# Attention and mixture kernel on one core: adding DMAs in the first quads, sums placed later, new drain counts, 33 plain steps

## Chip, core and metric

One core of a Trainium2 chip runs the whole program. The time is device microseconds of one execution, the median of several; a profiled execution of the same program gives the trace. The engines are TensorE (PE, with its weight loads PEld), VectorE (DVE), ScalarE (ACT), GpSimd (POOL) and SyncE (SP, which here only issues DMAs).

## What is computed

```python
B, N, C = 4, 6080, 256                    # q, k, v: [B, N, C], f32
qn = q / (norm(q, axis=1) + 1e-6); kn = k / (norm(k, axis=1) + 1e-6)
s = kn.transpose(0, 2, 1) @ qn / tau      # [B, C, C], a sum over all N tokens
a = softmax(s)                            # over the last axis
x = (v @ a).reshape(B * N, C)
h = x @ w_in                              # 256 -> 2048
out = (h - tanh(h)) @ w_out               # 2048 -> 256, f32
```

## The kernel before

The softmax matrix of a batch is folded into `w_in`, so the work on the tokens is (v times the folded weights), then h - tanh(h), then `w_out`. Each f32 operand is split into a high and a low part, and a product is three matmuls (high x low, high x high, low x high).

The tokens of a batch are taken in 6 pairs of column blocks (512 + 512, one pair 512 + 448), and the 2048 hidden channels in 8 slices of 256. One pair and one slice is a **quad**: a 2 x 2 product done by a seven-product scheme (`p1` to `p7`, banks X, Y, Z, tiles `x`, `y`, `z` in the trace). There are 4 x 6 x 8 = 192 quads, numbered `gs` from 0. A quad of the name `b_p_s` is batch, pair, slice. From a product TensorE hands a PSUM bank to ScalarE (`keep`, tiles `p1`, `u2`, `u3`), VectorE adds (`add`, tiles `c11`, `c22`, `c12`), ScalarE takes tanh, the tanh is subtracted (`sub`, or `join`), ScalarE casts the high part (`gh`), VectorE subtracts for the low part (`gl`), and TensorE multiplies with `w_out` (`second`, tiles `ps_o`).

How far these second products trail is `lag`: `ORDER`, `UNEVEN` and `HALVES` give the order of the seven products in a quad, and after each the number of second matmuls that are drained there. The quads of the last batch except its first pair (`halved`, `gs` 152 to 191) do also the first output column by a seven-product scheme on half blocks of 256 columns (tiles `ps_h`, sums `ts`, parts `b1`, `b2`, `t1`, `t2`); their banks Y and Z are the same one, so that `p5` (into Y) has to wait until VectorE has added `c11` out of Z. The sums of `w_out` for it (`Sums`, `plan_sums`) are made beforehand, eight of them, at quads `SUMS_AT` to `SUMS_AT + 7`.

Where `joined` says so, the subtraction is no VectorE instruction: ScalarE takes tanh(-h), and GpSimd issues a DMA that adds h onto it in SBUF (`join`). In the kernel before these are hidden blocks 11 and 12 of the 40 halved quads, 80 DMAs.

The inputs `w_in` and `w_out` are 64-bit floats; `Convert` turns a slice into a high and a low f32 part, with an addition `add` on the way (GpSimd's at first, VectorE's where `alone`: slices 1 to 7 of `w_out` and slice 7 of `w_in`).

The scores of batch 0 are done at the start by plain f32 matmuls (`score`), of the later batches by split matmuls, in units of one token tile and one half of the channels (`score_unit`). Of batch 1 the first `FILLS` of 48 token tiles are done by plain matmuls too (tiles `ps_s<-qh` and `ps_s<-ql`), put by the planner where TensorE would wait; the rest are units, six per quad at most (`PER`), in quads 17 to 22.

All instructions are recorded in a `Plan`; a list scheduler with costs written in the kernel (`order`) decides the order on each engine, and the program then runs in that order, in order on each engine. The planner takes a join to cost 1.0 on GpSimd and to be seen 4.5 plus 0.19 later (`JOIN_LAG`).

Of the kernel before, what the change touches and what calls it, by code (L numbers as in the profile page):

```python
# [15 lines left out]
ALU = mybir.AluOpType  # L16
AX = mybir.AxisListType

P = 128
# [22 lines left out]
UNEVEN = [  # L42
    ("p6", [2]), ("p2", ["c"]), ("p5", []), ("p7", [12]), ("p3", ["a"]), ("p4", ["d", 3]), ("p1", ["b", 7]),
]
HALVES = [
    ("p6", []), ("p2", [5, "c"]), ("p5", []), ("p7", [5]), ("p4", ["d", 3]), ("p3", ["a", 4]), ("p1", ["b", 5.5]),
]
HALF = NMAX // 2
LAST = 1
SHARE = 1  # L50
JOINED = [(),(11,12)]
SUMS_AT = 3 * 8
ENTER = 10
EARLY = 6
FILLS = 35
FILL_EVERY = 0.6
LEAD = 10
KEPT = 50.0
# [189 lines left out]
def act_cost(n):  # L248
    return 0.09 + n * 0.00084


def dve_cost(n):
    return 0.068 + n * 0.001042


def pool_cost(n):
    return 0.27 + n * 0.0022


def pe_cost(n):  # L260
    return 0.0134 + n * 0.000417
# [3 lines left out]
def attn_moe(ctx: ExitStack, tc: tile.TileContext, qk, v4, qkT, tau, w_in, w_out, outT):  # L265
# [6 lines left out]
    nc = tc.nc  # L272
    B, N, _, C = qk.shape
# [8 lines left out]
    while s0 < N:  # L282
        n = min(NMAX, N - s0)
# [24 lines left out]
    def sb(pool, tag, shape, dtype, name):  # L308
        return pool.tile(list(shape), dtype, tag=tag, name=name, bufs=ring[tag].bufs)

    def bank(i, name, shape=(P, 512)):

        return ps_p.tile(list(shape), F32, tag=f"bank{i}", name=name)
# [38 lines left out]
    class Convert:  # L352
# [29 lines left out]
            nc.vector.scalar_tensor_tensor(self.mf, self.low.bitcast(U32), 2.0 ** -52, self.mf, op0=ALU.mult, op1=ALU.mult)  # L382

        def add(self, eng):
            eng.tensor_add(self.af, self.af, self.mf)

        def hi(self):
            nc.scalar.copy(self.h, self.af)
# [116 lines left out]
    while j < NJ:  # L505
        n = min(GJ, NJ - j) if j else NJ % GJ or GJ
# [13 lines left out]
    def units_of(left):  # L520
        return [(m, g, jj) for m in range(KC) for g in [*left[:1], *left[-1:], *left[1:-1]] for jj in range(groups[g][1])]
# [4 lines left out]
    class Attn:  # L526
        def __init__(self, b):
# [9 lines left out]
            self.half, self.unit = {}, {}  # L537
            self.units = units_of(range(steps[FILLS][0] if b == SWEEP else 0, len(groups)))

# [59 lines left out]
        def score(self, g, jj):  # L599
# [4 lines left out]
            for m in range(KC):  # L604
                products(
                    self.ps[:, m, :], [((x[:, K_COLS[m]], None), (x[:, Q_ALL], None))],
                    first=i == 0 and m == 0, last=i == (FILLS if self.b else len(steps)) - 1 and m == KC - 1,
                )
# [349 lines left out]
    plan = Plan()  # L958
# [101 lines left out]
    def plan_convert(conv, dst, after=(), due=None, alone=False):  # L1060

        adds = ("DVE", dve_cost(WN), nc.vector) if alone else ("POOL", pool_cost(WN), nc.gpsimd)
        raw, c, t = Buf(ring["raw"]), Buf(ring["nt"]), Buf(ring["ob"])
        plan.add("SP", 0.35, conv.load, writes=[raw, dst], after=after, size=0.52, due=due)
        plan.add("ACT", act_cost(WN), conv.magnitude, reads=[raw], writes=[c])
        plan.add("DVE", 1.07, conv.upper, reads=[raw], writes=[c])
        plan.add("DVE", 1.06, conv.lower, reads=[raw, c], writes=[t])
        plan.add(*adds[:2], lambda: conv.add(adds[2]), reads=[t], writes=[c])
        plan.add("ACT", act_cost(WN), conv.hi, reads=[c], writes=[dst])
        plan.add(*adds[:2], lambda: conv.lo(adds[2]), reads=[c], writes=[dst])  # L1070

# [2 lines left out]
    def plan_w_in(s, due=None, after=(), alone=False):  # L1074
        w = wbuf[0, s] = Buf(ring["wi"])
        plan_convert(convert_w_in(s), w, after, due, alone)
        w.writers[-1].due = plan.pe_time - 0.5
        if s > EARLY:
            plan_keep(s, w)
        return w  # L1080
# [25 lines left out]
    def halved(b, p):  # L1106

        return b == B - 1 and p > 0
# [7 lines left out]
    class Quad:  # L1116
# [185 lines left out]
            stream.append((self, i))  # L1302

        def joined(self, i):
            return self.b == B - 1 and i in JOINED[halved(self.b, self.p)]

        def product(self, name):
            if name == "p1":
# [113 lines left out]
    def second(quad, i):  # L1422

        if isinstance(i, str):
            yield from second_halves(quad, i)
            return
        b, p, s = quad.b, quad.p, quad.s
        row, c = i // 10 - 1, i % 10 - 1
        n = quad.ns[c]
        f = 2 * s + row  # L1430
        gh, gl = quad.bufs["g", i]
        key = b, p, c
        first = key not in obufs
        if first:
            obufs[key] = [0] + [Buf(3 + 2 * c + m) for m in range(KC)]
        done = obufs[key]
        done[0] += 1
        last = done[0] == 2 * NS2

        parts = (0, 1, 0, 0), (0, 0, 0, 1), (1, 1, 0, 0), (1, 0, 0, 1), (1, 0, 1, 2), (0, 0, 1, 2)  # L1440
        end = last and b == B - 1 and p == NP - 1
        if end:
            parts = parts[0:2] + parts[5:6] + parts[2:5]
        for m, part, x, j in parts:
            def run(m=m, part=part, x=x, j=j):
                if first and j == 0:
                    outs[key + (m,)] = bank(3 + 2 * c + m, f"ps_o_{b}_{p}_{c}_{m}")
                nc.tensor.matmul(  # L1448
                    outs[key + (m,)][:, 0:n], (wo_l if part else wo_h)[:, f, m * P:(m + 1) * P], quad.g[i][x],
                    start=first and j == 0, stop=last and j == 2, skip_group_check=True,  # L1450
                )

            plan.add("PE", pe_cost(n), run, reads=[gl if x else gh, wobuf[s]], writes=[done[1 + m]])
            yield 1
        if last:
            at_ = b * N + pairs_of[b][p][0] + c * quad.ns[0]
            for m in range(KC):
                halves = b == B - 1
                ob = Buf(ring[("t" if halves else "raw") if c else "ob"])
                tiles = {}  # L1460

                def copy(m=m, tiles=tiles):
                    if halves:
                        tag = "t" if c else "ob"
                        tiles[0] = sb(g_p, tag, [P, NMAX], F32, f"ob_{b}_{p}_{c}_{m}")[:, 0:n]
                    elif c:
                        raw = sb(qk_p, "raw", [P, GJ, 2, C], F32, f"ob_{b}_{p}_{c}_{m}")
                        tiles[0] = raw[:, 0].rearrange("p x c -> p (x c)")[:, 0:n]
                    else:
                        tiles[0] = sb(g_p, "ob", [P, NMAX], F32, f"ob_{b}_{p}_{c}_{m}")[:, 0:n]  # L1470
                    (nc.scalar.copy if m else nc.vector.tensor_copy)(tiles[0], outs[key + (m,)][:, 0:n])  # L1471

                def store(m=m, tiles=tiles):
                    nc.sync.dma_start(outT[m * P:(m + 1) * P, at_:at_ + n], tiles[0])

                plan.add("ACT" if m else "DVE", act_cost(n) if m else dve_cost(n), copy, reads=[done[1 + m]], writes=[ob])
                plan.add("SP", 0.35, store, reads=[ob], size=0.26, due=plan.pe_time + 8.0)


    ats = {}  # L1480
# [2 lines left out]
    def task(gs, place, what):  # L1483
        beside.setdefault((gs, place), []).append(what)
# [162 lines left out]
    adds = 0  # L1647
# [12 lines left out]
    def plain_step(b, i, due=None):  # L1660
        g, jj = steps[i]
        if jj == 0:
            plain_load(b, g)

        return plan.add("PE", 2 * KC * 0.215, lambda: ats[b].score(g, jj), reads=held[b, g], writes=[scores[b]], due=due, fill=b == 1)
# [36 lines left out]

    fills = [plain_step(1, i, after_scores + FILL_EVERY * i) for i in range(FILLS)]

# [40 lines left out]
    for s in range(NS2):  # L1745
        task(SUMS_AT + s, "start", lambda s=s: plan_sums(s))
    for gs in range(halves_from, TOTAL):
# [17 lines left out]
    lag = LAG  # L1765
# [19 lines left out]
    for gs in range(TOTAL):  # L1785
        quad = quads.pop(gs)
        for what in beside.get((gs, "start"), ()):
            what()
        before, uneven = uneven, quad.ns[0] != quad.ns[1]
        if halves_from - 4 <= gs < halves_from:  # L1790
            lag += 3
        if gs == halves_from:
            lag += 2
        if before and not uneven:
            lag += ENTER if gs < halves_from else 0
            stream[-2:] = reversed(stream[-2:])
        for name, then in UNEVEN if uneven else HALVES if halved(quad.b, quad.p) else ORDER:
            if uneven and not before and name in ("p2", "p5"):
                drain(ENTER // 2)
            if name == "p1":  # L1800
                if gs + 1 < TOTAL:
                    quads[gs + 1] = Quad(gs + 1)
                    quads[gs + 1].product("p1")
            else:
                quad.product(name)
            for x in then:
                if not isinstance(x, str):
                    held = min(lag, x * SHARE if gs >= halves_from else x)
                    lag, x = lag - held, x - held
                    drain(x)  # L1810
                else:
                    for what in beside.get((gs, x), ()):
                        what()
# [66 lines left out]
```

## Time and profile before

| | us |
|---|---|
| time, median of 3 (lowest to highest) | 2145.12 (2145.1 to 2145.46) |
| time of the profiled execution | 2144.87 |
| its span, first to last instruction | 2143.1 |
| TensorE busy in it | 2135.9 |
| mean granted TensorE clock | 1.000 of 2.4 GHz |

The time holds 1.8 us that the span does not, and the profiled execution is 0.25 us under the median. Rows of the chain of work give a start, a length and what ran; rows of the timeline give start, length, engine, line, operation and, in brackets, the idle time of the engine before it with what ended it. Matmuls overlap, so the length of one matmul row says less than the distance between two starts.

### The profile page before, as it was taken

The numbers are of one execution on the slowest core, as the hardware profiler recorded it, in microseconds if no ns is written. First come the engines' busy times: TensorE is split into PE (matmuls) and PEld (weight loads), VectorE is DVE, ScalarE is ACT, GpSimd is POOL, SyncE is SP. The second block draws the span as 40 slices with busy tenths as digits, with TensorE's granted clock in tenths as the row PEclk, the third lists the DMA queues.
The fourth block names the chain that finished last, engine by engine and source line by source line (L and its number), as shares of the span: only waits on it lengthen the run. The fifth ranks groups of instructions, "written<-read, shape, count | busy, mean of one in ns | idle before, by whom it ended". The sixth has DMA issues, their size and how long they took to land.

```text
span 2143.1 us, 29494 instructions
## 1 busy us (share of the span) xinstructions
PE 2135.9 (100%) x10026; PEld 1802.5 (84%) x10026; DVE 1879.0 (88%) x3332; ACT 1616.3 (75%) x3015; POOL 106.2 (5%) x117
## 2 busy tenths in 40 slices
PE   9999999999999999999999999999999999999999
PEld 8888888888888888888888888888888888888887
DVE  8998988998898888888899888888888998988987
ACT  6677878767777787886777788887676777777776
POOL 5100000000000000000000000000000011111111
PEclk9999999999999999999999999999999999999999
DMA  9845676555335575643533567564353467877874
GB/s 384 303 165 194 214 253 222 189 181 184 127 135 187 212 245 212 219 162 108 199 138 126 180 231 246 196 227 158 110 197 125 156 207 204 230 230 205 231 209 136
DMA packets 143897, 419.73 MB, mean 196 GB/s; under 512 B 20674, under 2 KB 62914, under 8 KB 140674
## 3 DMA queue, kind: packets, MB, share of 16 engines
q1 hardware_dynamic: 132226, 396.87, 52.5%
q0 software_dynamic: 11520, 20.98, 5.4%
q8 instruction: 79, 1.29, 0.2%
q14 instruction: 72, 0.59, 0.1%
HBM read 329.19 MB, written 66.85 MB: 185 GB/s over the span
## 4 chain that ended last, share of the span: by engine, by line
PE 99%; DMA 1%; DVE 0%; SPq 0%; ACT 0%; issue 0%; ACTq 0%
PE ps_o L1448 43%; PE x L326 25%; PE y L326 12%; PE z L326 7%; PE ps_h L1371 5%; PE ps_s L326 3%; PE ps_s L653 2%; PE ps_s L651 1%; PE ps_w L326 1%; DMA n<-c 0%; DMA vhl<-qk_dram 0%; DVE c L1161 0%; DVE t L1285 0%; DVE v L955 0%; DVE gl L1293 0%
## 5 line engine op out<-in xcount | busy, mean ns | idle before, releaser
L326 PE MATMUL x<-v,f 128*128 128x512 f32 (+1 forms) x2304 | 628.2, 389 | 0.0
L1448 PE MATMUL ps_o<-gh,wo_h 128*128 128x512 f32 (+1 forms) x1376 | 533.6, 388 | 0.0
L1448 PE MATMUL ps_o<-gh,wo_l 128*128 128x512 f32 (+1 forms) x1376 | 533.5, 388 | 0.0
L326 PEld LDWEIGHTS x<-v,f 128*128 128x128 f32 x2304 | 430.1, 188 | 84.5
L1293 DVE TENSOR_TENSOR gl<-t,gh 128x512 fp32r<-128x512 f32 (+1 forms) x688 | 456.1, 679 | 20.9 <-ACT gh L1289 19.9
L1289 ACT CAST gh<-t 128x512 fp32r<-128x512 f32 (+1 forms) x688 | 412.2, 617 | 34.4 <-DVE t L1285 20.9
L1448 PE MATMUL ps_o<-gl,wo_h 128*128 128x512 f32 (+1 forms) x1376 | 428.0, 388 | 0.0
L1278 ACT ACTIVATE t<-c 128x512 f32<-128x512 f32 x536 | 333.8, 625 | 94.2 <-DVE c L1161 85.1
L1285 DVE TENSOR_TENSOR t<-c,t 128x512 f32<-128x512 f32 (+1 forms) x496 | 333.9, 677 | 24.7 <-ACT t L1278 19.5
L1151 ACT COPY u<-x 128x512 f32<-128x512 f32 (+1 forms) x384 | 221.9, 578 | 163.0 <-PE x L326 159.4
L1161 DVE TENSOR_TENSOR c<-u,y 128x512 f32<-128x512 f32 (+1 forms) x384 | 258.9, 674 | 76.3 <-ACT u L1151 47.9
L326 PE MATMUL y<-v,f 128*128 128x512 f32 (+1 forms) x1152 | 320.6, 387 | 1.1 <-DVE c L1161 1.0
L1448 PEld LDWEIGHTS ps_o<-gh,wo_l 128*128 128x128 f32 x1376 | 258.5, 188 | 51.4 <-DVE ob L1471 0.9
L1448 PEld LDWEIGHTS ps_o<-gl,wo_h 128*128 128x128 f32 x1376 | 258.2, 188 | 51.7 <-DVE gl L1293 0.6
L1448 PEld LDWEIGHTS ps_o<-gh,wo_h 128*128 128x128 f32 x1376 | 258.4, 188 | 49.1
L326 PEld LDWEIGHTS y<-v,f 128*128 128x128 f32 x1152 | 210.2, 188 | 36.2 <-DVE c L1161 1.8
L1161 DVE TENSOR_TENSOR c<-p,z 128x512 f32<-128x512 f32 x192 | 131.7, 686 | 36.3 <-PE z L326 33.5
L326 PE MATMUL z<-v,f 128*128 128x512 f32 x576 | 162.2, 390 | 0.0
L1278 ACT ACTIVATE t<-x 128x512 f32<-128x512 f32 x152 | 90.9, 598 | 92.7 <-PE x L326 91.1
L1285 DVE TENSOR_TENSOR t<-x,t 128x512 f32<-128x512 f32 x152 | 104.9, 690 | 45.4 <-ACT t L1278 44.9
L326 PEld LDWEIGHTS z<-v,f 128*128 128x128 f32 x576 | 108.1, 188 | 23.3 <-DVE t L1285 0.2
L1151 ACT COPY p<-x 128x512 f32<-128x512 f32 x192 | 112.7, 587 | 15.3 <-PE x L326 12.5
(215 smaller groups left out, 2191.4 us busy)
## 6 DMA issues: line engine op xcount, KB each, us to landing
f<-f_d SPq DMA_DIRECT2D x160, 896.0 KB, 4.6
raw<-qk_dram SPq DMA_DIRECT2D x104, 384.0 KB, 5.0
nt<-qkT_dram SPq DMA_DIRECT2D x96, 380.0 KB, 5.1
f_d<-f SPq DMA_DIRECT2D x32, 896.0 KB, 3.9
vraw<-v_dram SPq DMA_DIRECT2D x24, 1024.0 KB, 7.9
outT_dram<-ob SPq DMA_DIRECT2D x88, 256.0 KB, 3.2
sl<-so_d SPq DMA_DIRECT2D x40, 512.0 KB, 3.3
wt<-wt_d SPq DMA_DIRECT2D x24, 512.0 KB, 6.8
```

The source lines that it names most:

```text
L326: ins = nc.tensor.matmul(out, w, x, start=first and i == 0, stop=last and i == len(seq) - 1, skip_group_check=True,)
L651: nc.tensor.matmul(self.ps[:, 0:C], x[:, 1, k], x[:, 0, q], start=False, stop=last, skip_group_check=True)
L653: nc.tensor.matmul(self.ps.rearrange("p (a c) -> p a c", a=2), x[:, 0, k], x[:, :, q], start=first, stop=False, skip_group_check=True,)
L1151: nc.scalar.copy(self.tiles[to], self.tiles["X"][:, 0:n])
L1161: nc.vector.tensor_add(self.tiles[i], self.tiles[u], self.tiles[ps][:, 0:n])
L1278: nc.scalar.activation(self.tiles["t", i], self.tiles[c][:, 0:n], AF.Tanh, scale=-1.0 if apart else 1.0)
L1285: nc.vector.tensor_sub(x, self.tiles[c][:, 0:n], x)
L1289: nc.scalar.copy(self.g[i][0], self.tiles["t", i])
L1293: nc.vector.tensor_sub(self.g[i][1], self.tiles["t", i], self.g[i][0].bitcast(F32))
L1371: nc.tensor.matmul(outs[b, p, place][:, at_ * HALF:(at_ + 1) * HALF], weights(a, part), quad.g[name][x][:, half * HALF:(half + 1) * HALF], ...
L1448: nc.tensor.matmul(outs[key + (m,)][:, 0:n], (wo_l if part else wo_h)[:, f, m * P:(m + 1) * P], quad.g[i][x], start=first and j == 0, stop ...
```

## The change

It sets three tables anew (`HALVES`, `SUMS_AT` from quad 24 to quad 80, `FILLS` from 35 to 33), withholds one second matmul more at the first halved quad (`lag += 3` for `+= 2`), makes blocks 11 and 12 of quads 0 to 7 joined (16 DMAs more), makes the addition of the eight `alone` conversions an adding DMA (8 more), and lets ScalarE issue the store of the output block that it copied last.

```diff
-HALVES = [
-    ("p6", []), ("p2", [5, "c"]), ("p5", []), ("p7", [5]), ("p4", ["d", 3]), ("p3", ["a", 4]), ("p1", ["b", 5.5]),
-]
+HALVES = [("p6",[]),("p2",[5.5,"c"]),("p5",[]),("p7",[5.0]),("p4",["d",2.5]),("p3",["a",4]),("p1",["b",5.5])]
-SUMS_AT = 3 * 8
+SUMS_AT = 80
-FILLS = 35
+FILLS = 33
...
         def add(self, eng):
-            eng.tensor_add(self.af, self.af, self.mf)
+            if eng is None:
+                nc.gpsimd.dma_start(self.af, self.mf, accum_op=ALU.add)
+            else:
+                eng.tensor_add(self.af, self.af, self.mf)
...
+        far = alone and True
...
-        plan.add(*adds[:2], lambda: conv.add(adds[2]), reads=[t], writes=[c])
+        if far:
+            plan.add("POOL", 1.0, lambda: conv.add(None), reads=[t], writes=[c], port=False, lag=plan.JOIN_LAG)
+        else:
+            plan.add(*adds[:2], lambda: conv.add(adds[2]), reads=[t], writes=[c])
...
-            return self.b == B - 1 and i in JOINED[halved(self.b, self.p)]
+            return i in (JOINED[halved(self.b, self.p)] if self.b == B - 1 else (11,12,) if self.gs < 8 else ())
...
-                plan.add("SP", 0.35, store, reads=[ob], size=0.26, due=plan.pe_time + 8.0)
+                if end and m:
+                    plan.add("ACT", 0.1, lambda store=store: store(nc.scalar), reads=[ob])
+                else:
+                    plan.add("SP", 0.35, store, reads=[ob], size=0.26, due=plan.pe_time + 8.0)
...
         if gs == halves_from:
-            lag += 2
+            lag += 3
```

The tables go through the scheduler, so that what moves is seen only in the order of the instructions. ScalarE's rows in the first quad, before, from the tanh of block 11 (`t11_0_0_0`) to the cast of its high part (`gh11_0_0_0`):

```order
L1278 ACTIVATE t11_0_0_0_782<-c11_0_0_0_769 128x512
L1151 COPY u3_0_0_0_786<-x_0_0_0_728 128x512
L388 CAST wo_h_95<-a_wo3_714 128x512
L1278 ACTIVATE t22_0_0_0_797<-c22_0_0_0_791 128x512
L1278 ACTIVATE t21_0_0_0_810<-x_0_0_0_728 128x512
L1289 CAST gh11_0_0_0_815<-t11_0_0_0_782 128x512
```

The same stretch of ScalarE now (lines from 1156 on are five higher, and `u3_0_0_0` stands one row ahead of these):

```order
L1283 ACTIVATE t11_0_0_0_776<-c11_0_0_0_763 128x512
L891 CAST f_2_782<-fx_0_2_758 128x896
L1283 ACTIVATE t22_0_0_0_789<-c22_0_0_0_780 128x512
L1283 ACTIVATE t21_0_0_0_798<-x_0_0_0_718 128x512
L367 ACTIVATE a_wo4_803<-raw_wo4_676 128x512
L1156 COPY p1_0_0_1_809<-x_0_0_1_791 128x512
L1294 CAST gh22_0_0_0_812<-t22_0_0_0_789 128x512
L1294 CAST gh21_0_0_0_819<-t21_0_0_0_798 128x512
L1283 ACTIVATE t12_0_0_0_829<-c12_0_0_0_817 128x512
L1156 COPY u2_0_0_1_835<-x_0_0_1_791 128x512
L1294 CAST gh11_0_0_0_844<-t11_0_0_0_776 128x512
```

The cast of block 11 stands nine instructions behind its tanh where it stood four behind, and the second matmuls of block 11 are still the first on TensorE. VectorE's rows at the second halved quad (`3_1_1`) before, from the first that reads its joined block (`n11_3_1_1`) to the addition `c11` of the quad after:

```order
L1234 TENSOR_TENSOR ts_3_1_1_18131<-n11_3_1_1_18056 128x256
L1234 TENSOR_TENSOR ts_3_1_1_18131<-n21_3_1_1_18105,n11_3_1_1_18056 128x256
L1285 TENSOR_TENSOR t22_3_1_1_18136<-c22_3_1_1_18080,t22_3_1_1_18136 128x512
L1214 TENSOR_TENSOR glb1_3_1_1_18156<-n11_3_1_1_18056,ghb1_3_1_1_18145 128x256
L1214 TENSOR_TENSOR t1_3_1_1_18150<-ts_3_1_1_18131,t1_3_1_1_18150 128x512
L1161 TENSOR_TENSOR c11_3_1_2_18169<-p1_3_1_2_18127,z_3_1_2_18152 128x512
```

The same place on VectorE now:

```order
L1239 TENSOR_TENSOR ts_3_1_1_18149<-n11_3_1_1_18072 128x256
L1290 TENSOR_TENSOR t22_3_1_1_18151<-c22_3_1_1_18099,t22_3_1_1_18151 128x512
L1219 TENSOR_TENSOR glb1_3_1_1_18171<-n11_3_1_1_18072,ghb1_3_1_1_18160 128x256
L1239 TENSOR_TENSOR ts_3_1_1_18149<-n21_3_1_1_18121,n11_3_1_1_18072 128x256
L1166 TENSOR_TENSOR c11_3_1_2_18182<-p1_3_1_2_18144,z_3_1_2_18167 128x512
```

The same waiting row heads the stretch, and one subtraction of 512 columns (`t1`) has gone behind `c11_3_1_2`. TensorE's rows where the second quad of the halved stage ends, before, with the second products on half blocks as `ps_h`:

```order
L326 MATMUL x_3_1_1_18002<-v5_3_1_17883,f_153_17831 128x512 x3
L1448 MATMUL ps_o_3_0_1_0_17273<-gl12_3_0_7_17980,wo_h_95 128x448
L1371 MATMUL ps_h_3_1_3_18090<-glb1_3_1_0_18029,wo_h_95 128x256
L1371 MATMUL ps_h_3_1_3_18090<-ghb1_3_1_0_18020,wo_h_95 128x256
L1371 MATMUL ps_h_3_1_3_18090<-ghb1_3_1_0_18020,wo_l_96 128x256
L326 MATMUL y_3_1_1_18058<-v6_3_1_17896,f_153_17831 128x512 x3
```

And now:

```order
L324 MATMUL x_3_1_1_18019<-v5_3_1_17901,f_153_17849 128x512 x3
L1453 MATMUL ps_o_3_0_1_1_17296<-gl12_3_0_7_17998,wo_h_95 128x448
L1453 MATMUL ps_o_3_0_1_0_17291<-gl12_3_0_7_17998,wo_h_95 128x448
L1376 MATMUL ps_h_3_1_3_18111<-glb1_3_1_0_18045,wo_h_95 128x256
L324 MATMUL y_3_1_1_18074<-v6_3_1_17914,f_153_17849 128x512 x3
L1376 MATMUL ps_h_3_1_3_18111<-ghb1_3_1_0_18037,wo_h_95 128x256
L1376 MATMUL ps_h_3_1_3_18111<-ghb1_3_1_0_18037,wo_l_96 128x256
```

A run of 256-column matmuls is cut in two by the product `y`; so it is in every halved quad but the last ones, and a quad has five such runs (of 1, 2, 5, 11 and 2 matmuls) where it had four (of 3, 7, 10 and 1).

Elsewhere: between quads 23 and 151 TensorE's order is the same. The plain steps that go are those of the tile `ql_17`, which stood at the end of quads 6 and 7 (and the load of that tile, 512 KB); four units (a 512-column and a 256-column matmul each) come in quads 17 to 22. On SP the stores `wi_d3` to `wi_d5` stand some rows later. At the first halved quad one second matmul of 512 columns, which stood between `z` and `y`, now stands behind `y`.

## Rows read from the trace of the kernel before

**Rows 1.** The page: busy us (share) and instructions; the chain by engine.

```profile
PE 2135.9 (100%) x10026; PEld 1802.5 (84%) x10026; DVE 1879.0 (88%) x3332; ACT 1616.3 (75%) x3015; POOL 106.2 (5%) x117
...
PE 99%; DMA 1%; DVE 0%; SPq 0%; ACT 0%; issue 0%; ACTq 0%
```

**Rows 2.** Who waited for whom, TensorE: us in total, times, longest.

```profile
PE y L326 <- DVE c L1161: 1.0, 1, 1.0
```

**Rows 3.** Timeline of the last microseconds.

```profile
2138.22 0.39 PE L1448 MATMUL ps_o<-gl,wo_h 128*128 128x512 f32 x1
...
2139.26 0.84 SPq L1474 DMA_DIRECT2D outT_dram<-ob  x2
```

**Rows 4.** Windows: us, busy PE, PEld, DVE, ACT, POOL; clock, DMA share, GB/s.

```profile
85.00:95.00 10.00, 10.00 (x51) 8.58 (x50) 9.93 (x19) 8.34 (x16) 0.00 (x0) 1.00 1.02 420
...
2139.00:2140.00 1.00, 0.00 (x0) 0.00 (x0) 0.01 (x1) 0.23 (x1) 0.00 (x0) 1.00 1.04 404
...
1736.00:1746.00 10.00, 10.00 (x48) 8.50 (x47) 7.99 (x16) 6.80 (x14) 1.72 (x2) 1.00 1.01 320
```

**Rows 5.** The chain in time, a plain step and four units.

```profile
166.54 0.86 PE ps_s L326 x4
...
252.91 0.91 PE ps_s L653 x4
253.82 0.47 PE ps_s L651 x4
```

**Rows 6.** The chain in quads 33 to 35, second matmuls.

```profile
437.17 2.03 PE ps_o L1448 x8
...
443.37 2.04 PE ps_o L1448 x9
...
447.68 1.81 PE ps_o L1448 x8
...
453.57 2.19 PE ps_o L1448 x9
```

**Rows 7.** VectorE by line, 340 to 450 us: one of six rows of a sum.

```profile
L471 DVE TENSOR_TENSOR so<-wo_h,wo_l 128x512 f32<-128x512 f32 x8 | 5.5, 684 | 0.0
```

**Rows 8.** The chain at the second and third halved quads.

```profile
1739.99 0.28 issue
1740.28 7.21 DMA n<-c
...
1749.21 0.60 DVE t L1214
1749.81 0.61 DVE c L1161
...
1750.47 0.96 PE y L326 x3
```

**Rows 9.** Timeline of TensorE and its weight loads at the halved quads.

```profile
1729.53 0.30 PEld L326 LDWEIGHTS y<-v,f 128*128 128x128 f32 x2 [0.55 <-DVE c L1161]
...
1747.42 0.85 PE L326 MATMUL z<-v,f 128*128 128x512 f32 x3
```

**Rows 10.** The chain in a quad of the halved stage.

```profile
1901.95 0.69 PE y L326 x3
...
1904.61 0.68 PE x L326 x3
...
1906.56 0.93 PE ps_o L1448 x4
```

**Rows 11.** Timeline of the first quads: tanh of block 11, its first matmul.

```profile
83.88 0.63 ACT L1278 ACTIVATE t<-c 128x512 f32<-128x512 f32 x1
...
91.75 0.39 PE L1448 MATMUL ps_o<-gh,wo_l 128*128 128x512 f32 x1
```

**Rows 12.** The 80 joins, by line: issue to landing (first `t`, then `n`).

```profile
DMA to landing us min/median/max: 3.2/4.2/8.8
...
DMA to landing us min/median/max: 3.3/3.8/7.2
```

**Rows 13.** DMA issues from 77 to 87 us: count, KB, median us to landing.

```profile
wi_d<-wi SPq DMA_DIRECT2D x6, 512.0 KB, 9.1
...
raw_wi<-w_in_dram SPq DMA_DIRECT2D x1, 512.0 KB, 11.3
```

More of the change, by code (lines that the diff above doesn't have):

```diff
@@ L1471, in copy, with store @@
                     (nc.scalar.copy if m else nc.vector.tensor_copy)(tiles[0], outs[key + (m,)][:, 0:n])
-                def store(m=m, tiles=tiles):
-                    nc.sync.dma_start(outT[m * P:(m + 1) * P, at_:at_ + n], tiles[0])
+                def store(queue=nc.sync, m=m, tiles=tiles):
+                    queue.dma_start(outT[m * P:(m + 1) * P, at_:at_ + n], tiles[0])
                 plan.add("ACT" if m else "DVE", act_cost(n) if m else dve_cost(n), copy, reads=[done[1 + m]], writes=[ob])
-                plan.add("SP", 0.35, store, reads=[ob], size=0.26, due=plan.pe_time + 8.0)
+                if end and m:
+                    plan.add("ACT", 0.1, lambda store=store: store(nc.scalar), reads=[ob])
+                else:
+                    plan.add("SP", 0.35, store, reads=[ob], size=0.26, due=plan.pe_time + 8.0)
     ats = {}
```

## The prediction

> **What bounds the kernel now.** I read the page first, its busy times and its chain of work. TensorE is busy 2135.9 of a span of 2143.1 us, and the chain that ended last is 99% TensorE [rows 1]. VectorE is busy 88% of the span, ScalarE 75%, and both only matter where TensorE waits for one of them. So the end is set by TensorE's own work, and all that is not that work is 2143.1 - 2135.9 = 7.2 us: the start, the tail and the stalls. A change can win by taking matmuls away or by closing a stall, and it loses by adding matmuls or opening one.
>
> Then the view of who waited for whom. It lists one stall of TensorE in the middle of the program with a size: product `y` waits 1.0 us, once, for a `c` of VectorE [rows 2]. The chain names the place, the third halved quad, and what is ahead of the stall there: a join that landed 7.21 us after its issue, then VectorE [rows 8]. A second, smaller gap is at the first halved quad, where the weight load of a `y` stood idle 0.55 before VectorE's `c` came [rows 9]. Smaller ones still don't appear as waits; I find them by the length of equal runs: eight second matmuls in a row take 1.81 us in one place and 2.03 in another [rows 6]. The last matmul starts at 2138.22, and the two stores on SP's queue that follow begin at 2139.26 [rows 3]. The windows give the share of the DMA engines that the transfers want at the places of the change [rows 4]. The last thing I read is the start: when the first quad's tanh is done and when TensorE wants the result [rows 11].
>
> **The change part by part.**
>
> *Plain steps.* Two steps of 0.86 go. Four units come: in the chain the four 512-column matmuls of four units take 0.91, the four of 256 columns 0.47, together 1.38 [rows 5]. 2 x 0.86 = 1.72 away, 1.38 added: **-0.34**. TensorE has no idle time at either place that would hide this, and the order of the matmuls between is the same, so I keep it whole.
>
> *The sums.* One is 2 x 0.684 and some short rows, about 2.5 us of VectorE by the six rows of which the group shows the first; eight of them are 20 us [rows 7]. They stood in quads 24 to 34, and there the runs of second matmuls are stretched: 2.03 for 1.81, and 2.19 for nine where another run of nine took 2.04 [rows 6]. That is 0.22 + 0.15, so **-0.37** if the stretch comes from the sums. It could be 0 (the stretch has another cause), and at the new place in quads 81 to 90 the same 20 us of VectorE could cost up to the same 0.37 again. I take the full gain, since VectorE is less loaded at the new place.
>
> *The halved stage.* At the second halved quad VectorE's row `ts` waits for the join, and everything behind it in order waits too, `c11` of the next quad last, for which `y` stands still 1.0. One 512-column subtraction (0.60, [rows 8]) no longer lies between the two. The join is as late as before, so 0.6 of the 1.0 goes: -0.6. It would be all of it, -1.0, if the join came a little sooner; nothing, if `ts`, now in another order, ends as late as before. Against that the one more withheld second matmul at the first halved quad takes 1.81 / 8 = 0.226 of cover from between `z` and `y`, where the weight load already waited for `c` [rows 6, 9]: +0.23. Together **-0.37**, from -1.0 to +0.3. The transfer of cover is real work behind `y`, so nothing else comes of it.
>
> *The drains.* Each halved quad has one run of 256-column matmuls more. The sum of the counts is the same, so no matmul is added; the price is a change of shape and of the PSUM bank. A run of three 512-column matmuls takes 0.69 where it stands behind such a change and 0.68 where not, and a run of four 0.93 for 4 x 0.226 = 0.90 [rows 6, 10]. So one change of run costs between 0 and 0.03; I take the difference that is in the same shape, 0.01, for 39 quads: **+0.4**, from 0 to 1.2.
>
> *The first quads.* Sixteen subtractions, two in each of quads 0 to 7, leave VectorE and become transfers, and so do eight additions. VectorE gains nothing that TensorE can see, since no stall on VectorE stands there. What counts is when the first block lands. The tanh of block 11 ends at 83.88 + 0.63 = 84.51 [rows 11]; the copy `u3` now stands ahead of it, about 0.6 by the 0.63 of the tanh, and plain work of TensorE that stood ahead of the products now stands behind them, which takes some of that back (the matmuls ahead of the first `ps_o` are as many as before); I put the end at 84.8, half way. The issue follows 0.28 later, as at the third halved quad [rows 8]: 85.1. TensorE's first second matmul wants block 11 at 91.75, and the cast before it takes about as long as the tanh, 0.63. With 0.05 from VectorE's end to the product in [rows 8] as the handing over, the block must land by 91.07, that is 6.0 after the issue. The 80 joins of before took 3.2 to 8.8, with medians of 4.2 and 3.8 [rows 12]. The long ones are those with a full queue of transfers beside them: the join of 7.21 lies in a window with a DMA share of 1.01, and the window from 85 to 95 has 1.02 [rows 4, 8]. So I take 7.21: landing at 92.31, cast to 92.94, first second matmul at 92.99, **+1.2**. Below, it is 0 for every latency up to 6.0. Above: the transfers issued on SP between 77 and 87 landed after 9.1 in the median (`wi_d`) and 11.3 (`raw_wi`) [rows 13]; a join that waits as long as the longest lands at 96.4, +5.3. The later 15 joins have the same wait ahead of them once TensorE has been pushed back, so only one that is later than its forerunner adds to it; from 7.21 to the 8.8 of the worst that would be 1.6, and I count nothing. Behind the waiting instructions on GpSimd's queue stand only other joins and, later, one slice's conversion, which nothing needs for some quads. On ScalarE, what is queued behind the waiting cast `gh11` are the tanhs and copies of the next quad; they would wait 1.2 with TensorE, not beyond it.
>
> The conversions themselves I price at nothing: VectorE's addition of 0.68 gives way to a transfer of a few us, and the slices of `w_out` it feeds are wanted one quad after the other, far later. What covers them is this lead; without it one would cost as the first join does.
>
> *ScalarE's store.* After the last matmul four blocks leave the chip. In the window from 2139 to 2140 the DMA engines already have a share of 1.04 [rows 4], with the stores on SP's queue 0.84 for two [rows 3]. An issue that is earlier on another queue moves bytes that wait for the same engines: **0**, between -0.3 and +0.3 (a third of those 0.84). The Trainium skill, in "Trainium Kernel Development and Optimization", Key Constraints, says that DMAs issued from several engines run on the same 16 DMA engines and interleave, so that only issue time is saved; by that rule it is nil too, and no run here has such a store yet.
>
> **The sum.** -0.34 - 0.37 - 0.37 + 0.4 + 1.2 + 0 = +0.5. The profiled execution took 2144.87, which gives 2145.4; the median of the runs is 0.25 above it, so **2145.6**.
>
> **The rivals.**
>
> *The first joins land in time* (chance 0.32). Latency 6.0 or less, as most of the 80. For it: the medians of 3.8 and 4.2. Against it: they come from stretches with a quiet queue. Then the term of 1.2 is nil: 2144.4. The Trainium skill, "DMA: Bandwidth & Descriptors", Anatomy of one DMA, gives for a DMA of GpSimd's software path about 2.0 us plus the bytes at 436 GB/s; an estimate from it for 256 KB is 2.6, with which this rival would hold. The trace has 3.2 at the least and 8.8 at the most, so here it is a floor.
>
> *The joins stand behind the whole backlog of SP* (chance 0.12), the other side. A join is a small transfer among 512 KB loads that took 9.1 to 11.3 [rows 13]. If it waits for them as they wait for each other, latency 11.3, then +5.3 in place of +1.2: 2149.7, slower by 0.21%. It decides from a latency of about 11.0, where 2149.4 is reached, 4.3 above the median. Against it: no join took over 8.8, and at a share of 1.01 one took 7.21.
>
> *The change does not do what it says at the stalls* (chance 0.04): VectorE ends `c11` as late as before, the sums were not the cause of the stretch. Then 0.37 + 0.6 are lost, the sum is +1.5, and the time 2146.6.
>
> **How the numbers follow.** My forecast, a wait of some 0.5 to 3 us at the first join and small gains elsewhere, has 0.52. The lower end, 2143.4, is the in-time rival with both stalls of the halved stage gone and no cost of the drains (2144.4 - 0.6 - 0.4); the upper end, 2148.6, is a latency of 10.2, some way to the backlog. About 2 in 10 are left out, most of it above. A measurement of this kernel can tell about 0.2%, 4.3 us, from no change. All that could be won is the 1.0 at `y`, the 0.37, the 0.34 and some tenths, so faster by that much has 0.01. Slower needs the backlog rival at full size or more joins late one behind the other: 0.07, a part of its 0.12. The same: 0.92.
>
> **What would show it.** Right: TensorE waits about 1.2 near 92 us, for ScalarE's cast behind a join with 6 to 8 from issue to landing; in the chain the runs of eight second matmuls in quads 33 to 35 take 1.81; the wait of `y` at the third halved quad is about 0.4 and at the first grows by about 0.2; a halved quad is longer by some hundredths. Wrong: no wait near 92 (then 2144.4), or one of several us; a new wait at quads 81 to 90, which would take the gain of the sums back; or a last store on ScalarE that lands well before SP's did, which would show that the tail was not full.

## The result, and the profile after

The changed kernel takes 2158.23 us (median of 4, 2157.58 to 2163.01), the kernel before 2145.11 in the same runs: the ratio is 1.0067, 95% interval 1.0055 to 1.0078. That is 13.1 us slower, outside the range. The profiled execution is the longest of the four, 2163.01, 4.8 above the median; so places and mechanisms are read from its trace, and what a part costs is taken from medians.

The page's busy times, and the view of who waited for whom on TensorE (us in total, times, longest), of the changed kernel:

```profile
PE 2141.9 (99%) x10026; PEld 1803.3 (83%) x10026; DVE 1871.6 (87%) x3312; ACT 1618.2 (75%) x3019; POOL 127.8 (6%) x141
```

```profile
PE x L324 <- ACT fx L815: 4.6, 3, 2.4
PE x L324 <- ACT u L1156: 3.3, 3, 2.6
PE ps_o L1453 <- ACT ob L1476: 2.6, 4, 1.7
PE x L324 <- ACT p L1156: 2.3, 4, 0.9
```

The wait of `y` for `c` [rows 2] is gone from the list; in its place stand four kinds of wait, all on ScalarE, which is busy 75% as before. So it is not short of time; something stands in its line. All waits of TensorE, with those of the start, come to 14.7 us, 2.6 before. That is 12.1 of the 18.1 by which the span is longer (2161.2 beside 2143.1); the other 6.0 are TensorE's busy time, for the same 10026 matmuls. The chain from 76 us on names the first thing that stands in line (start, length, what ran; `...` marks rows left out):

```profile
76.32 9.63 DMA a_wo<-m_wo
...
85.97 0.62 ACT wo_h L389
```

The same on ScalarE's timeline (idle time before a row in brackets, with what ended it), and on TensorE's:

```profile
81.75 0.57 ACT L1156 COPY u<-x 128x512 f32<-128x512 f32 x1
85.97 0.62 ACT L389 CAST wo_h<-a_wo 128x512 fp32r<-128x512 f32 x1 [3.65 <-DMA a_wo<-m_wo]
86.49 0.83 ACT L815 ACTIVATE fx<-ps_w,rs 128x256 f32<-128x256 f32 x2
87.22 0.58 ACT L1156 COPY u<-x 128x512 f32<-128x512 f32 x1
```

```profile
87.85 1.66 PE L324 MATMUL x<-v,f 128*128 128x512 f32 x6 [2.61 <-ACT u L1156]
...
114.72 0.96 PE L324 MATMUL x<-v,f 128*128 128x512 f32 x3 [2.38 <-ACT fx L815]
...
129.32 0.96 PE L324 MATMUL x<-v,f 128*128 128x512 f32 x3 [2.00 <-ACT fx L815]
```

The addition of a slice of `w_out` is a transfer that lands 9.63 us after its issue. Nobody wants the slice yet, but its cast `wo_h` stands in ScalarE's line, and behind it the copy `u` that frees a bank: TensorE stands 2.61 at 87.85. The other two of these stalls stand behind something else: the cast `gh` of a joined block, which waits for its join, and behind it on ScalarE the rows `fx` for which TensorE waits:

```profile
112.80 0.62 ACT L1294 CAST gh<-t 128x512 fp32r<-128x512 f32 x1 [1.97 <-DMA t<-c]
113.32 0.47 ACT L815 ACTIVATE fx<-ps_w,rs 128x256 f32<-128x256 f32 x1
...
128.28 0.62 ACT L1294 CAST gh<-t 128x512 fp32r<-128x512 f32 x1 [1.58 <-DMA t<-c]
128.80 0.47 ACT L815 ACTIVATE fx<-ps_w,rs 128x256 f32<-128x256 f32 x1
```

So conversions and first joins hold ScalarE's line in the same way. The transfers of this stretch, 70 to 160 us (count, KB, median us to landing):

```profile
t<-c POOLq DMA_DIRECT2D x12, 256.0 KB, 6.8
...
a_wo<-m_wo POOLq DMA_DIRECT2D x7, 256.0 KB, 6.7
```

In the halved stage a second picture. ScalarE and TensorE at the second halved quad, timeline of the changed kernel:

```profile
1756.17 0.62 ACT L1294 CAST gh<-t 128x512 fp32r<-128x512 f32 x1 [3.17 <-DMA t<-c]
1756.69 0.59 ACT L1190 ACTIVATE t<-x 128x512 f32<-128x512 f32 x1
1757.18 0.52 ACT L1476 COPY ob<-ps_o 128x448 f32<-128x448 f32 x1
```

```profile
1757.76 0.51 PE L1453 MATMUL ps_o<-gh,wo_l 128*128 128x512 f32 x1 [1.74 <-ACT ob L1476]
```

The cast of joined block 12 (its transfer: 8.51 us) holds the copy `ob` that frees a bank of the second products. The same three rows of the kernel before stand the other way round:

```profile
1742.09 0.53 ACT L1471 COPY ob<-ps_o 128x448 f32<-128x448 f32 x1
1742.77 0.60 ACT L1185 ACTIVATE t<-x 128x512 f32<-128x512 f32 x1
1744.93 0.62 ACT L1289 CAST gh<-t 128x512 fp32r<-128x512 f32 x1 [1.56 <-DMA t<-c]
```

There the same cast waits too, but what TensorE needs has gone ahead of it. And after some long stalls the clock is down. Windows of the changed kernel behind the stall at 1757.76 (the columns as in [rows 4]):

```profile
1757.00:1758.00 1.00, 0.24 (x1) 0.19 (x1) 0.69 (x2) 0.70 (x2) 0.00 (x0) 1.00 1.03 396
1758.00:1759.00 1.00, 1.00 (x5) 0.77 (x5) 1.00 (x3) 0.62 (x1) 0.00 (x0) 0.90 0.98 375
1759.00:1760.00 1.00, 1.00 (x4) 0.81 (x3) 1.00 (x3) 0.86 (x2) 0.00 (x0) 0.50 0.94 217
```

The granted clock stays at 0.50 (1.2 GHz) for three such windows and is back at 1.00 in 1763 to 1764. A second such stretch lies behind the stall at 129.32.

What the change was to gain is there: the chain in quads 33 to 35 has no stretched run any more, where [rows 6] had 2.03 and 2.19.

```profile
449.26 1.81 PE ps_o L1453 x8
...
455.16 2.04 PE ps_o L1453 x9
```

### The profile page after: what moved, and what is told of

The parts are those of the page before. It is cut to its first block, busy times and chain, and to the rows that moved or that the text cites. A ratio compares the mean times of both kernels' runs of the same rounds, so it can differ in the third digit from the quotient of the medians.

```text
span 2161.2 us, 29597 instructions
## 1 busy us (share of the span) xinstructions
PE 2141.9 (99%) x10026; PEld 1803.3 (83%) x10026; DVE 1871.6 (87%) x3312; ACT 1618.2 (75%) x3019; POOL 127.8 (6%) x141
## 4 chain that ended last, share of the span: by engine, by line
PE 67%; issue 26%; DMA 4%; POOL 2%; ACT 1%; DVE 0%; SPq 0%; POOLq 0%; ACTq 0%
PE ps_o L1453 30%; PE x L324 17%; PE y L324 8%; PE z L324 4%; DMA t<-c 3%; PE ps_s L324 3%; PE ps_h L1376 2%; PE ps_s L654 2%; PE ps_s L652 1%; DMA a_wo<-m_wo 1%; POOL t L1286 1%; POOL n L1181 1%; DMA vhl<-qk_dram 0%; ACT gh L1294 0%; DMA outT_dram<-ob 0%
## 5 line engine op out<-in xcount | busy, mean ns | idle before, releaser
L1453 PE MATMUL ps_o<-gl,wo_h 128*128 128x512 f32 (+1 forms) x1376 | 422.1, 388 | 0.0
L1290 DVE TENSOR_TENSOR t<-c,t 128x512 f32<-128x512 f32 (+1 forms) x480 | 324.4, 678 | 26.1 <-ACT t L1283 20.5
```

The lines of the kernel that those rows point to most:

```text
L1290: nc.vector.tensor_sub(x, self.tiles[c][:, 0:n], x)
L1453: nc.tensor.matmul(outs[key + (m,)][:, 0:n], (wo_l if part else wo_h)[:, f, m * P:(m + 1) * P], quad.g[i][x], start=first and j == 0, stop ...
```

## The experiments

Theory **A** for the first quads: a cast on ScalarE that waits for an adding transfer holds what stands behind it. Its rivals are the joins in place of the conversions (**B**), and too much traffic in sum (**C**). Theory **D** for the halved stage: the place of block 12's cast on ScalarE. Its rivals: the counts do as predicted (**E**), or they leave TensorE without cover (**H**).

**Without the conversions' transfers**, `e1_vector_additions`:

```diff
-        far = alone and True
+        far = False
```

> The changed kernel with the eight additions of the conversions back on VectorE; the sixteen joins of the first quads stay. Theory A (a conversion's transfer that lands after 6.3 to 9.6 us holds the cast wo_h on ScalarE, and the folding and the copies queued behind it): the start of quad 8, 11.75 us later than in the kernel before, is at most 4 us later, and the time falls from 2158.2 to 2150.5 or less. Rival B (the joins of the first quads hold ScalarE in the same way): the time stays above 2154. Rival C (each alone fits into the DMA engines' capacity and only both together do not): about 2147.

**Without the joins of the first quads**, `e2_no_first_joins`, and **with neither**, `e3_no_early_dmas`:

```diff
-            return i in (JOINED[halved(self.b, self.p)] if self.b == B - 1 else (11,12,) if self.gs < 8 else ())
+            return i in (JOINED[halved(self.b, self.p)] if self.b == B - 1 else ())
```

> The changed kernel without the sixteen joins of quads 0 to 7; the additions of the conversions stay adding transfers. Theory A: the cast wo_h still waits, the first stall near 87 us (2.6 us of TensorE) stays, the time is above 2152. Rival B: 2149 or less. Rival C: about 2147.

> The changed kernel with neither the joins of the first quads nor the adding transfers of the conversions; sums, plain steps, drains and ScalarE's store as changed. All of A, B and C: quad 8 starts within 0.5 us of where it does in the kernel before; what is left is the halved stage, 2145 plus 1.5 to 6 us, so 2146 to 2151. If it is 2144 to 2145, the halved stage's stalls in the changed kernel came out of the late start of the transfers, and not out of the drains.

Measured: 2152.41 without the conversions' transfers (ratio to the kernel before 1.0036, 1.0024 to 1.0049), 2163.72 without the joins (1.0091, 1.0077 to 1.0105), 2155.80 with neither (1.0052, 1.0039 to 1.0064). The conversions cost 2158.23 - 2152.41 = 5.8. But A's number for the first run (2150.5 or less) was missed, B's (above 2154, then 2149 or less) and C's (2147) were met in neither of the first two, and the run with neither is above what any theory allowed. It has no stall of size in the first quads (TensorE is busy 99.81 of the 100 us from 80 to 180); it has one of 5.9 at 273 us that the changed kernel does not have. The run without the joins keeps the first stall, as A says (2.09 at 88.02), and has a stall on `ob` like that one too, 5.19 at 281 us. The chain of the run with neither:

```profile
263.04 6.31 DMA outT_dram<-ob
...
269.36 3.34 DMA raw<-qk_dram
...
272.73 0.51 ACT unit L637
273.24 0.49 ACT ob L1476
...
273.77 4.10 PE ps_o L1453 x10
```

A load of a score tile waits for a store to land, its cast `unit` waits for the load, and the copy `ob` that TensorE needs stands behind the cast. With the joins taken out the scheduler writes another order here. So a part taken out of this change is not only its own cost, and I looked next for which part gives that order.

What the run without the conversions shows of the joins alone (its chain, then ScalarE's and TensorE's timeline):

```profile
84.50 8.74 DMA t<-c
```

```profile
93.26 0.62 ACT L1294 CAST gh<-t 128x512 fp32r<-128x512 f32 x1 [2.68 <-DMA t<-c]
```

```profile
93.97 0.47 PE L1453 MATMUL ps_o<-gh,wo_l 128*128 128x512 f32 x1 [2.34 <-issue]
```

**Single parts put into the kernel before**: the sums (`SUMS_AT = 80`), the plain steps (`FILLS = 33`), ScalarE's last store, each alone.

> The kernel before with the eight sums at quad 80 alone. Theory F (as in the changed kernel, where the start of the quads came 0.59 us less late from quad 33 to 36): faster by 0.5 to 0.6 us, 2144.3 to 2144.5, no new stall in quads 81 to 92. Rival: the gain came of the shifted transfers there, and the time does not move.

> The kernel before with 33 plain steps alone. On ScalarE a copy ob of quad 16's pair then stands behind the casts of three more score tiles, as in the run without early DMAs, where TensorE stood 5.9 us before it. Theory G (this order is the cause of that stall, and the joins of the first quads only happen to give another order): slower by 6 to 8 us. Rival (the stall came with the sums or with the start's transfers): faster by 0.3 to 0.4 us, as predicted.

> The kernel before with ScalarE's last store alone. As predicted: no change, between 0.3 us faster and 0.3 us slower, the window after the last matmul with a DMA share of about 1.0 in both. Rival: the earlier issue is worth its 0.3 to 0.4 us on SP's queue.

The sums: 2144.02 beside 2144.72 (0.9997, 0.9988 to 1.0006), too little to tell from none by the times, but the runs of second matmuls are all at 1.81 and 2.04 and the trace has no new wait in quads 81 to 92. The store: 2144.94 beside 2145.13 (1.0001, 0.9992 to 1.0010), nothing. The plain steps alone: 2152.94, **8.2 us slower** (1.0039, 1.0026 to 1.0051), a little over the 6 to 8 of theory G, and the same stall on `ob` at quad 17 is there:

```profile
267.32 0.36 PE L1448 MATMUL ps_o<-gh,wo_l 128*128 128x448 f32 x1
267.52 0.36 PE L1448 MATMUL ps_o<-gh,wo_h 128*128 128x448 f32 x1
273.42 0.74 PE L1448 MATMUL ps_o<-gh,wo_l 128*128 128x448 f32 x1 [5.53 <-ACT ob L1471]
...
275.45 0.57 PE L1448 MATMUL ps_o<-gh,wo_h 128*128 128x448 f32 x1
275.82 0.57 PE L1448 MATMUL ps_o<-gh,wo_l 128*128 128x448 f32 x1
```

Theory G held: with 33 plain steps the scheduler puts `ob` behind casts of more score tiles. In the changed kernel, and in the run without the conversions' transfers, that stall is not there, in the run without the joins it is; so in these orders the joins shift `ob` ahead of the casts again. They do not always do so, as the next run shows. Behind the stall the matmuls come 0.37 apart, not 0.20 as at 267.32 and 267.52: the granted clock is 0.50 there.

**The conversions, with the planner told that they land late**, `e8_later_conversions`, which keeps the transfers and moves only the casts:

```diff
-            plan.add("POOL", 1.0, lambda: conv.add(None), reads=[t], writes=[c], port=False, lag=plan.JOIN_LAG)
+            plan.add("POOL", 1.0, lambda: conv.add(None), reads=[t], writes=[c], port=False, lag=10.0)
```

> The changed kernel with one number of the planner changed: a conversion's adding transfer is taken to be seen 10.0 us later in place of 4.5. The same transfers; the casts wo_h stand further back on ScalarE. Theory A (the cast that waits on ScalarE is what a conversion costs): most of the 5.8 us between the changed kernel and the run with VectorE's additions is back, 2152 to 2154. Rival I (it is the traffic on full DMA engines, by which other transfers land later): 2157 or more.

The time is 2161.49 (1.0078, 1.0066 to 1.0091): by the time alone rival I. The trace says why the time does not decide here. It has the stall on `ob` at quad 17 again, 5.2 at the longest, and a window shows the first quads apart from it (80 to 180 us; first the changed kernel, then this run):

```profile
80.00:180.00 100.00, 91.45 (x415) 73.78 (x414) 82.22 (x145) 69.95 (x129) 21.72 (x24) 0.98 0.81 233
```

```profile
80.00:180.00 100.00, 95.71 (x445) 78.87 (x444) 87.57 (x154) 75.23 (x140) 22.11 (x25) 1.00 0.84 249
```

TensorE is idle 8.6 of 100 us in the changed kernel and 4.3 here, with the same transfers and a DMA share no lower; without the conversions' transfers it was 3.2 (busy 96.77). The conversions' transfers are as slow as in the changed kernel (median 6.8, there 6.7), but ScalarE waits for none of them any more, where it had five such waits there, 9.9 us in all. So most of the conversions' loss went with the place of the cast, as theory A has it, and traffic is at most a small rest.

**The drains.** The new counts with the one more withheld matmul, `e4_drains_only`; then the same with the planner told that joins of a pair's first three quads land after 7.0, `e7_drains_later_casts`; the counts alone (`lag += 2`), `e9_counts_only`; the withheld matmul alone (`lag += 3`), `e10_withheld_only`; and the first with block 12 on VectorE, `e11_block12_on_vector`:

```diff
-JOINED = [(),(11,12)]
+JOINED = [(),(11,)]
```

> The kernel before with the new drain counts and the one more withheld second matmul alone. Theory D (the cast of joined block 12 now stands ahead of the copy that frees a second bank and of a tanh on ScalarE, so a join of 7.5 to 8.5 us holds these): slower by 1.5 to 6.5 us, TensorE waiting for a copy ob or a copy u at the first quads of a pair. Rival E (the drains are as predicted, and the stalls come of something else): faster by 0.2 to 1.0 us, with the wait of y at the third halved quad shorter by about 0.6.

> The run with the drains alone, with one number of the planner changed: joins of the first three quads of a pair are taken to be seen 7.0 us later in place of 4.5. TensorE's order is the same; on ScalarE the cast of block 12 of the first halved quad stands behind the copy ob and the tanh of block 21, not ahead of them. Theory D (that place of the cast is the cause of the stalls): the slowdown of 3.6 us falls below 1, perhaps to a gain of up to 1, and the waits of TensorE for ob are gone. Rival H (the counts themselves, less cover between the products, make TensorE wait at the first quads of a pair, wherever the cast stands): still slower by 2 us or more.

> The kernel before with the new drain counts alone, without the one more withheld second matmul. ScalarE's order at the first halved quads is that of the kernel before (the cast of block 12 behind the copy ob and the tanh of block 21). Theory D (that order decides): no stall on ob, and a gain of 0.1 to 0.6 us, from 0.008 us less in each of some 36 quads as the run with the drains alone shows them. Rival H (the counts leave the products without cover): slower by 2 us or more.

> The kernel before with one second matmul more withheld at the first halved quad, and the counts as they were. ScalarE's order there is that of the changed kernel. Theory D: the stalls on ob and u at the first quads of a pair are back, slower by 2.5 to 5 us. Rival H: no change beyond 0.5 us.

> The run with the drains alone (counts and one more withheld), with block 12 of the halved quads subtracted by VectorE instead of joined, so that its cast waits for no transfer. Theory D: the stalls on ob at the first quads of a pair are gone; VectorE has 40 x 0.6 us more to do and may wait elsewhere, so between 1 us faster and 2 us slower than the kernel before. Rival H: slower by 3.6 us or more, stalls on ob at the same quads.

| run | us | ratio to the kernel before (interval) |
|---|---|---|
| drains alone | 2148.56 | 1.0018 (1.0009 to 1.0026) |
| casts later | 2148.32 | 1.0017 (1.0008 to 1.0026) |
| counts alone | 2145.83 | 1.0004 (0.9995 to 1.0013) |
| withheld alone | 2149.55 | 1.0023 (1.0013 to 1.0033) |
| drains, block 12 on VectorE | 2142.78 | 0.9990 (0.9981 to 0.9998) |

The withheld matmul gives the whole loss, the counts none that can be measured, though no gain either. And the loss is the join's: without it the same tables are 2.35 us faster than the kernel before (2145.13 in that comparison), more than the 1 us that D had allowed. Block 12 on VectorE with the old tables was not run, so how much of that gain is the tables' and how much the missing join's stays open. TensorE's waits with the withheld matmul alone, and then with block 12 on VectorE (the whole list; both rows there are of the start):

```profile
PE ps_o L1448 <- ACT ob L1471: 2.1, 2, 1.8
```

```profile
PE idle L1821 <- DVE ones L316: 1.1, 1, 1.1
PE ps_s L324 <- DMA vhl<-qk_dram: 0.5, 1, 0.5
```

The longer of the two waits, 1.8, ends at 1745.44, and the clock behind it is down as in the changed kernel (withheld matmul alone, the columns as in [rows 4]; the next 5 us have 0.98):

```profile
1745.00:1750.00 5.00, 4.56 (x16) 3.78 (x17) 4.18 (x8) 2.95 (x6) 0.86 (x1) 0.68 0.91 319
```

That is 1.7 us of matmul time, so stall and clock make 3.5 of the 4.0 by which that span is longer than the one before.

The run with later casts is the miss: its wait on `ob` is gone, as theory D says, but the time is not, since the new order has waits of `y` and of a copy `u` in other quads (1.8 and 1.7 us in all). So D is shown by e9, e10 and e11, and H falls with them; e7 alone would have left it open.

**Three more**: the halved stage within the changed kernel, the joins at another place, and the parts that pay.

> The changed kernel with block 12 of the halved quads on VectorE in place of the join; everything else as changed. If the loss in the halved stage is the join of block 12 in the order that the one more withheld matmul gives, it falls by as much as between the runs with the drains alone with and without that join, 5.8 us: 2152.4, give or take 1. If the late start of the kernel or its other transfers made those stalls: less than 3 us.

> The kernel before with the joins of blocks 11 and 12 in quads 4 to 7 alone, eight transfers in a stretch where the DMA share was 0.3 to 0.6. Theory J (a first join costs by the queue of transfers that it lands in): within 0.6 us of the kernel before, latencies of 3 to 6 us, against 4.7 us for the sixteen of quads 0 to 7. Rival K (a joined block costs wherever it is, by the cast that stands in line on ScalarE): slower by 2 us or more.

> The kernel before with the sums at quad 80, the new drains with the one more withheld second matmul, and block 12 of the halved quads on VectorE: the parts that the runs so far show without a new stall, and none of the early transfers, with 35 plain steps. If the parts add up: 2.3 us from the drains without the join and 0.6 from the sums, 2142.1 to 2142.6, faster than both kernels. If VectorE, which has the sums and these subtractions in different quads, makes a new wait: above 2143.5.

The changed kernel with block 12 on VectorE takes 2153.54 (1.0039, 1.0027 to 1.0052): 4.7 of its loss was that join, just under the 4.8 to 6.8 that I had allowed, and in its trace TensorE waits nowhere in the halved stage. The eight joins in quads 4 to 7 cost 3.5 (2148.41; 1.0017, 1.0008 to 1.0026), so theory J missed its number and K's was met. In the trace one of the eight has a stall of its own, behind a transfer as slow as in quad 0:

```profile
135.71 8.37 DMA t<-c
...
144.10 0.03 ACT gh L1289
...
144.63 0.48 ACT fx L814
...
145.15 0.97 PE x L326 x3
```

The eight have a median of 5.4 to landing. K, a cost wherever a join is, asks for a loss at every one, and seven show no stall; so the trace speaks for the latency, as J has it, but the stretch was no quiet one at 144 (DMA share 0.89 from 140 to 146). This one run does not settle it. Another 0.7 lies in quad 16, where by the new order a unit waits for its scale on ScalarE. The two are 2.9 of the 3.5. The parts that pay, together: **2142.17 us** (2142.09 to 2142.48; 0.9987, 0.9978 to 0.9996), faster than both kernels, and close to the sum of its parts (2.75 us where they give 3.05).

## Why the prediction was wrong, step by step

- **"The conversions themselves I price at nothing ... What covers them is this lead."** This step failed. I asked when TensorE wants the slice, and not what stands behind its cast on ScalarE. They cost 5.8 of the 13.1, through ScalarE's line; the transfers took 6.7 in the median and up to 9.6. Not all of the 5.8 need be waits at their own casts: the waits of `x` for `fx` behind casts of joined blocks, 2.4 and 2.0 above, are at most 0.5 without them. How it divides is not shown.
- **The halved stage, -0.37.** Wrong in sign: the one more withheld matmul lost about 4 (the drains alone 3.6; the join of block 12 in the changed kernel 4.7). I followed VectorE's and TensorE's order and priced 0.23 of cover; the same number also moved ScalarE's cast of block 12 ahead of a bank's copy, and that I did not read: "nothing else comes of it" failed. The wait of `y` is gone from the changed kernel, but TensorE had been held 1.74 just before, which alone could cover it. With the counts alone it is still there (0.98), so they did not close it.
- **The first joins, +1.2.** The wait that it describes, at the first second matmul, is not in the changed kernel, where that matmul starts at 95.25 without idle time; the wait at 87.85, behind a conversion, came first. It is there without the conversions: the first join took 8.74, not 7.21, and TensorE stood 2.34 at 93.97. So for that case the mechanism was right and the term too small. That later joins add nothing was wrong: one of 7.48 at 96.23 and more followed. TensorE stood 0.21 and 0.54 more there at 105 and 111, and in the changed kernel 2.38 and 2.00 behind casts of joined blocks. From the medians, 2152.41 - 2144.93 is 7.5; less 3.6 for the drains and plus 0.7 and 0.34 for the gains, 4.9 is left for the joins. That is a remainder, not a measurement: the 0.34 was never measured, with 4.7 for block 12 it would be 3.8, and the trace shows 3.1.
- **The sums, -0.37.** Right in kind; the trace of the changed kernel has the full run lengths. By the medians 0.7, which the interval does not separate from none.
- **Plain steps, -0.34.** The count of the matmuls was right, and in the changed kernel no stall stands there. That the edit could cost 8.2 alone, by an order on ScalarE, I had not seen; in the changed kernel another order hid it.
- **The drains' counts, +0.4.** No cost that can be measured: 1.0004.
- **ScalarE's store, 0.** Right: alone it gives 1.0001. The windows behind the last matmul of the changed kernel, with stores on both queues, are full. The Trainium skill, "Trainium Kernel Development and Optimization", Key Constraints, says that queues of several engines share the 16 DMA engines; their share of 0.96 and 1.04 agrees with it:

```profile
2157.00:2158.00 1.00, 0.00 (x0) 0.00 (x0) 0.14 (x1) 0.37 (x1) 0.00 (x0) 1.00 0.96 371
2158.00:2159.00 1.00, 0.00 (x0) 0.00 (x0) 0.00 (x0) 0.00 (x0) 0.00 (x0) 1.00 1.04 404
```

- **The rivals.** The one on the other side, a first join that waits for the whole backlog, was nearest in time and not the cause: no join took 11.3, the longest of the changed kernel 9.3. The joins did not land in time either, and the sums were the cause of the stretch, which the third rival doubted. The estimate of 2.6 us from the Trainium skill, "DMA: Bandwidth & Descriptors", Anatomy of one DMA, had no transfer near it in the first quads: the medians there are 6.7 and 6.8, the least 3.2.

So about 5.8 of the loss are conversions, 3.6 to 4.7 the join of block 12 in its new place, and what is left, 3.8 to 4.9, the first joins, against some 1 us of gains. These terms come from runs whose orders differ elsewhere too; only the conversions and block 12 were each taken out of the changed kernel without bringing the stall at quad 17.

## What to carry to other kernels

A transfer that replaces an engine's instruction is paid where the next instruction waits for it in order: read what stands behind that instruction on its engine, and above all the copies that free banks, before calling a result not urgent. Price a transfer by the longest of its kind in a stretch with full DMA engines, and the more so where a planner schedules with one number for all of them (4.5 here, for 3.2 to 9.6). Where a scheduler makes the order, compare the order of every engine, not only of the two that the edit names, and expect that parts taken alone give orders that the whole never had.

## What the runs showed of the hardware

A stall of TensorE can cost more than its length. Behind the stalls of 1.74 and 5.53 the granted clock was 0.50 for 3 us and more after matmuls had started again, and 448-column matmuls came 0.37 apart in place of 0.20. In the changed kernel the windows 1758 to 1763 have 0.90, 0.50, 0.50, 0.50 and 0.90: 1.7 us of matmul time lost, as much as the stall ahead of it. The stall of 2.61 at 87.85 had no such sequel, nor had that of 2.38 at 114.72 or that of 1.0 in the kernel before, while that of 2.00 at 129.32 had one; what separates them these runs do not settle.
